# A fused attention and feed-forward kernel: w_out in two tiles, the first relu halved, one sum order exchanged, and fewer score turns in columns 1 and 2

## The chip, the cores and the metric

The kernel runs on one core of a Trainium2 chip. The metric is the device time of one execution in microseconds, the median of several runs. Besides the time there is a hardware profile: one execution with the start and the duration of every instruction on TensorE (PE; its weight loads are PEld), VectorE (DVE), ScalarE (ACT), GpSimd (POOL) and the issuing queues (SP is SyncE), and of every DMA packet.

## The reference

Eight batches of 3008 rows go through a gated attention without softmax, and its result through a feed-forward layer with the activation h cos h:

```python
# u, v: (8, 3008, 256); z: (8, 3008, 64); float32
scores = (1.0 / S) * np.matmul(z, z.transpose(0, 2, 1))
attn = np.maximum(scores, 0.0) ** 2
x = (u * np.matmul(attn, v)).reshape(B * S, D)
# w_in: (256, 2048), w_out: (2048, 256)
h = x @ w_in
out = (h * np.cos(h)) @ w_out
```

The scores are symmetric, because both factors are z.

## The kernel before

Each batch is cut into six columns of 512 rows (J = 0 to 5); the eight batches make 48 slots of one column each. A **score piece** (J, I) holds the 512 x 512 scores of column J against row block I, already through relu and square, as 128 partitions of 2048 fp16 elements. Since the scores are symmetric, piece (I, J) is the transpose of (J, I), and most pieces below the diagonal are not computed but **turned**: a transposing DMA, issued from SyncE, writes the transpose into another buffer. There are 18 such buffers, given out in a fixed order while the program is built.

A score group is two matmul blocks into one of three PSUM banks called E, a relu on ScalarE, and a square on VectorE that writes half a piece:

```python
    def emit_score(later=None):
        b, J, I, h = groups[done_groups[0]]
        ...
            nc.tensor.matmul(
                e[:, t, 0:Wt],
                zT[rows, k * P:(k + 1) * P],
                zT[rows, J * CW:J * CW + Wt],
                start=True,
                stop=True,
            )
        key = (b, J, I)
        a = new_piece(key) if h == 0 else piece(key)
        r = rpool.tile([P, 2, CW], FP16, name="r")
        nc.scalar.activation(r[:, :, 0:W], e[:, :, 0:W], AF.Relu)
        def square():
            ...
                a4 = a.rearrange("p (k w) -> p k w", w=CW)[:, 2 * h:2 * h + 2, 0:W]
                nc.vector.tensor_tensor(a4, r[:, :, 0:W], r[:, :, 0:W], ALU.mult)
        ...
        if cut or (I > J and (b, J, I) not in direct):
            turns.append(((b, I), key))
            turns.sort(key=lambda t: t[0])
            turn_slots[key] = pieces[key]
            pending[pieces[key]] = "held"
```

The list of turns is sorted by the column that will read the result. `emit_turns(due, more)` issues all turns for columns up to `due`, and `more` beyond that. A piece on the diagonal is turned in place by three small DMAs. The buffer of a turned piece is free for a new piece from then on, as soon as its DMA has read it:

```python
    def emit_turns(due, more=0):
        while turns and (turns[0][0] <= due or more > 0):
            if turns[0][0] > due:
                more -= 1
            (b, c), key = turns.pop(0)
            ...
            if I == J:
                ...    # three small transposing DMAs within the piece
            else:
                d = new_piece((b, I, J))
                nc.sync.dma_start_transpose(d.rearrange("p (n j) -> p n j", j=P), a)
            if pending.pop(i) == "dropped":
                free_pieces.append(i)
```

Columns 0, 1 and 2 of the first batch have a phase of their own, which computes all its pieces directly and issues one turn after each row block of columns 1 and 2:

```python
    def phase_a_first(s, n, extra={}):
        ...
            if dh > 0 and (k % 4 == 3):
                drop_piece((b, J, k // 4))
                if s > 0:
                    emit_turns((0, 0), 1)
                    if k < 4:
                        turn_u(s)
                    elif k < 8:
                        for d in range(2):
                            gate_mul(s - 1, d, late_sums.pop(0))
            for _ in range(at.get(i, 0)):
                emit_score(later=squares if s == 0 and i == lo else None)
        if s == 0:
            turn_u(0)
        late_sums.extend(gate_sum(s, *acc[dh]) for dh in range(2))
        hold(late_sums[0][0:1, 0:1])
        load_u(s + 1)
        e_order.append(ea)
```

`gate_sum` adds the two accumulators of one half of the 256 output columns: ScalarE copies one, VectorE adds the other. In column 0 the half dh = 0 is accumulated in the banks M, dh = 1 in a bank E.

From column 3 on, a slot is a `phase_a` (values of one column, with the scores of later columns between them) and a `phase_b` (the feed-forward projections h of the slot before, and the output products of the one before that). `phase_a` calls `emit_turns((b, J))` at its start and `emit_turns(<next column>, 1)` after each score; the `phase_b` after column 2 and all later ones issue one more turn at three places. All stores and all transposing DMAs stand in one queue, SyncE's:

```python
    for s in range(3, NSLOT + 1):
        ...
            phase_a(s)
        ...
            if J == (2 if b > 0 else 3):
                turn_z(b + 1, 1)
        ...
        if s < NSLOT - 2:
            turn_u(s + 2)
        phase_b(s)
```

The head of the kernel casts the first z to fp16, turns it on TensorE, and computes the first scores; filler matmuls keep TensorE going:

```python
    cast_z(nc.vector, 0)
    cast_z(nc.vector, 1)
    cast_z(nc.vector, 2)
    ...
    turn_on_pe(0)
    copy_turned(0)          # on ScalarE; the others on VectorE
    turn_on_pe(1)
    copy_turned(1)
    emit_score(later=squares)
    emit_score(later=squares)
    turn_on_pe(2)
    copy_turned(2)
    squares.pop(0)()
    squares.pop(0)()
    ...
    turn_on_pe(3)
    copy_turned(3)
    filler(2)
    emit_score()
    filler(1)
    emit_score()
    filler(1)
    ...
    phase_a_first(0, 12, {4: lambda: turn_late(4), 8: lambda: turn_late(5)})
    phase_a_first(1, 12)
    nc.gpsimd.dma_start(w_out16, moe_w_out.rearrange("(k p) f -> p k f", p=P))
```

Of the kernel before, what the change touches and what calls it, by code (L numbers as in the profile page):

```python
# [9 lines left out]
FP16 = mybir.dt.float16  # L10
# [4 lines left out]
def kernel(  # L15
# [9 lines left out]
    nc = tc.nc  # L25
    AF = mybir.ActivationFunctionType
# [36 lines left out]
    ppool = pool("ps", 1, space=bass.MemoryType.PSUM)  # L63

    w_in16 = kpool.tile([P, 2, Dff], FP16, name="w_in16")
    w_out16 = kpool.tile([P, NFT, D], FP16, name="w_out16")
    w_mix = kpool.tile([P, 4, NFT // 2, P], FP16, name="w_mix")
    s1, s2, s4 = (kpool.tile([P, NFT // 2, 2 * P], FP16, name=n) for n in ("s1", "s2", "s4"))
    warm = s1[:, 0:2, :].rearrange("p a b -> p (a b)")
# [117 lines left out]
    turn_slots = {}  # L187
    done_groups = [0]

    def emit_score(later=None):  # L190
        b, J, I, h = groups[done_groups[0]]
        done_groups[0] += 1
        cut = I == J and not (b == 0 and J < 3)
        W = 2 * P if cut and h == 0 else width(J)
        zT = zTs[b]
        e = E[take_e()]
        for t in range(2):
            k = 4 * I + 2 * h + t
            half = t if h == 0 else 1 - t
            rows = slice(half * H, (half + 1) * H)  # L200
            Wt = min(W, (2 * h + t + 1) * P) if cut else W
# [7 lines that stand above are left out]
        key = (b, J, I)  # L209
        a = new_piece(key) if h == 0 else piece(key)  # L210
        r = rpool.tile([P, 2, CW], FP16, name="r")
        nc.scalar.activation(r[:, :, 0:W], e[:, :, 0:W], AF.Relu)  # L212
        def square():
            if I > J:
                a4 = a.rearrange("p (k t j) -> p t k j", k=4, j=P)[:, 2 * h:2 * h + 2, :, :]
                r4 = r.rearrange("p t (k j) -> p t k j", j=P)
                nc.vector.tensor_tensor(a4, r4, r4, ALU.mult)  # L217
# [4 lines that stand above are left out]
        if later is None:  # L222
            square()
        else:
            later.append(square)
        if h == 0:
            return
# [11 lines that stand above are left out]
            b, J, I = key  # L239
            i = turn_slots[key]  # L240
            a = piece_bufs[i]
            if I == J:
                a4 = a.rearrange("p (k w) -> p k w", w=CW)
                for rr in range(1, 4):
                    rows = P if J * 4 + rr < NB - 1 else H
                    nc.sync.dma_start_transpose(
                        a4[:, 0:rr, rr * P:rr * P + rows],
                        a[0:rows, rr * CW:rr * CW + rr * P],
# [6 lines that stand above are left out]
# [19 lines left out]
    def gate_sum(s, b0, b1):  # L274
        W = width(s % NC)
        sm = spool.tile([P, CW], FP32, name="sm")
        nc.scalar.copy(sm[:, 0:W], b0[:, 0:W])
        nc.vector.tensor_tensor(sm[:, 0:W], b1[:, 0:W], sm[:, 0:W], ALU.add)  # L278
        return sm
# [75 lines left out]
    def phase_a_first(s, n, extra={}):  # L355
        b, J = s // NC, s % NC
        ea = e_order.pop(0)
        pair = [E[ea][:, 0, :], E[ea][:, 1, :]]
        acc = [pair, M] if s == 1 else [M, pair]
        last = NB - 1  # L360
        run = 1 if s == 0 else 2
        steps = [
            (dh, k)
            for I in range(0, NC, run)
            for dh in range(2)
            for k in range(4 * I, min(4 * (I + run), last))
        ] + [(2, last)]
        lo, hi = 5 if s == 0 else 2, 42
        at = {}
        for i in range(n):  # L370
            p = lo + (hi - lo) * i // (n - 1)
            at[p] = at.get(p, 0) + 1
        for i, (dh, k) in enumerate(steps):
            if i in extra:
                extra[i]()
            if dh == 2:
                emit_value(b, J, last, 0, 0, acc[0][0], False, True)
                emit_value(b, J, last, 1, 1, acc[1][1], False, True)
            else:
                for t in range(2):  # L380
                    emit_value(
                        b, J, k, t, dh, acc[dh][t], k == 0, k == last - 1 and t != dh
                    )
            if dh > 0 and (k % 4 == 3):
                drop_piece((b, J, k // 4))
                if s > 0:
                    emit_turns((0, 0), 1)
                    if k < 4:
                        turn_u(s)
                    elif k < 8:  # L390
# [3 lines that stand above are left out]
                emit_score(later=squares if s == 0 and i == lo else None)  # L394
        if s == 0:
            turn_u(0)
        late_sums.extend(gate_sum(s, *acc[dh]) for dh in range(2))
        hold(late_sums[0][0:1, 0:1])
        load_u(s + 1)
        e_order.append(ea)  # L400
# [51 lines left out]
            )  # L452

    def mix_weights():
        b11, b12 = w_out16[:, 0:F, 0:P], w_out16[:, 0:F, P:D]
        b21, b22 = w_out16[:, F:, 0:P], w_out16[:, F:, P:D]
        t = [w_mix[:, i, :, :] for i in range(4)]
        for dst, p, q in ((t[0], b12, b11), (t[1], b22, t[0]), (t[2], b22, b12), (t[3], b21, t[1])):
            nc.gpsimd.tensor_tensor(dst, p, q, ALU.subtract)
# [5 lines left out]
    def middle(m):  # L465
        acc = M[0][:, 0:D]
        for ft in range(NFT):
            nc.tensor.matmul(  # L468
                acc, gs[m][:, ft, P:T], w_out16[:, ft, :], start=(ft == 0), stop=(ft == NFT - 1)
            )  # L470
        nc.scalar.activation(y_outs[m][0][:, 1, :], acc, AF.Copy, bias=0.0, scale=inv_s2)

    def product(m, n, place):
# [2 lines left out]
        nk = nk // P  # L476
        t = lambda i: w_mix[:, i, :, :]
        left, right = {
            1: (g[:, 0:F, up], w_out16[:, 0:F, 0:P]),
            2: (g[:, F:, up], w_out16[:, F:, 0:P]),  # L480
            3: (s4, w_out16[:, F:, P:D]),
            4: (g[:, F:, low], t(3)),
            5: (s1, t(0)),
            6: (s2, t(1)),
# [46 lines left out]
    def y_block(m, ft, k):  # L531
        final = m == NSLOT - 1
        nc.tensor.matmul(  # L533
            y_bank(m, k),
            gs[m][:, ft, k * P:(k + 1) * P],
            w_out16[:, ft, :],
            start=(ft == 0 and (k % 2 == 0 or (final and k == 3))),
            stop=(ft == NFT - 1 and (k % 2 == 1 or k == mwidth(m) // P - 1 or (final and k == 2))),
        )
# [112 lines left out]
    def cast_z(eng, g):  # L652
        dst = z16s[0][:, 4 * g:4 * g + 4, :].rearrange("p k (t d) -> p k t d", t=2)
        eng.tensor_copy(dst, z32[g].unsqueeze(2).to_broadcast([P, 4, 2, dqk]))
# [7 lines left out]

    def copy_turned(g):
        dst = zTs[0][:, g * CW:(g + 1) * CW]
        if g == 0:
            nc.scalar.copy(dst, turned[g])
        else:
            nc.vector.tensor_copy(dst, turned[g])

    wc = cpool.tile([P, 2, CW], FP16, name="c")  # L670
    nc.scalar.activation(wc[:, 0, 0:P], warm[:, 0:P], AF.Sin)
# [1 line left out]
        nc.tensor.matmul(E[i % 2][:, 0, :], warm[:, 0:P], warm, start=True, stop=True)  # L673
    cast_z(nc.vector, 0)
    cast_z(nc.vector, 1)
    cast_z(nc.vector, 2)
    for g in range(3, NC):
        cast_z(nc.gpsimd, g)
        if g == 3:
# [1 line left out]
    squares = []  # L681
    turn_on_pe(0)
    copy_turned(0)
    turn_on_pe(1)
    copy_turned(1)
    emit_score(later=squares)
    emit_score(later=squares)
    turn_on_pe(2)
    copy_turned(2)
    squares.pop(0)()  # L690
    squares.pop(0)()
    M = [ppool.tile([P, CW], FP32, name=f"M{i}", tag=f"M{i}") for i in range(2)]

    def filler(n):
        for i in range(n):
            nc.tensor.matmul(M[1], warm[:, 0:P], warm, start=True, stop=True)  # L696

    turn_on_pe(3)
    copy_turned(3)
    filler(2)  # L700
    emit_score()
    filler(1)
    emit_score()
# [14 lines left out]

    phase_a_first(0, 12, {4: lambda: turn_late(4), 8: lambda: turn_late(5)})
    phase_a_first(1, 12)  # L720
    nc.gpsimd.dma_start(w_out16, moe_w_out.rearrange("(k p) f -> p k f", p=P))
    for i in range(2):
        emit_h(0, i)()
    phase_a_first(2, 14)
# [65 lines left out]
```

## Time and profile before

| | |
|---|---|
| median of 3 runs | 1193.03 us (1192.85 to 1193.06) |
| span of the profiled execution | 1191.2 us |
| TensorE busy | 1183.7 us, 99% |
| VectorE busy | 1011.5 us, 85% |
| ScalarE, GpSimd busy | 67%, 57% |
| SyncE's queue (turns, stores): time of its packets | 56.6% of 16 DMA engines |
| GpSimd's queue (loads with a cast): time of its packets | 27.7% of 16 DMA engines |

The span runs from the first to the last instruction of the profiled execution. A row of a timeline has the start, the duration, the engine, the line of the kernel, the operation, and the tiles written and read; rows of one group that follow each other are merged (x3). What stands in square brackets is the time that the engine stood idle before it, and what ended it. A row of the waits has the waiting engine and its line, what it waited for, the total, the number and the longest. Two rows of the page carry a digit for each of 40 equal slices of the span, of some 30 us each: the busy share in tenths.

### The profile page before, as it was taken

The page shows a single profiled execution, that of the slowest core. Times are in us where ns is not written, and L with a number is a line of the kernel's source. Part 1 is how long each engine was busy: PE and PEld are TensorE (multiplying, and loading weights), DVE is VectorE, ACT ScalarE, POOL GpSimd, SP SyncE. Part 2 cuts the span into 40 slices and gives each one's busy share as a digit, 9 for nine tenths or more (in the row PEclk, how much of TensorE's full clock was granted, in tenths as well). Part 3 has the DMA queues.
Part 4 walks back from the last instruction along what each step waited for, and adds up shares of the span by engine and source line. Part 5 has one row for each costly group of instructions (what it writes and reads, how often), then busy time and mean ns, then how long its engine had stood idle before and what let it go on. Part 6 is the DMA issues. An engine that isn't in the chain of part 4 may idle for free.

```text
span 1191.2 us, 29044 instructions
## 1 busy us (share of the span) xinstructions
PE 1183.7 (99%) x11887; PEld 726.8 (61%) x11887; DVE 1011.5 (85%) x1302; ACT 794.9 (67%) x927; POOL 679.0 (57%) x717
## 2 busy tenths in 40 slices
PE   9999999999999999999999999999999999999998
PEld 4556665665566656666566665656666566665566
DVE  6888888889988898888988889888888888888776
ACT  7966676667666676667676676666766666666454
POOL 3286745657466573755647556476555655545452
PEclk9999999999999999999999999999999999999999
DMA  9999999569995799955999469984798837974301
GB/s 160 175 172 158 115 171 130 102 122 104 173 127 101 123 137 166 126 89 103 155 152 130 86 106 158 168 123 70 120 162 152 122 72 120 173 122 84 65 20 54
DMA packets 449142, 148.00 MB, mean 124 GB/s; under 512 B 401264, under 2 KB 432496, under 8 KB 449008
## 3 DMA queue, kind: packets, MB, share of 16 engines
q1 hardware_dynamic: 368464, 112.93, 56.6%
q0 software_dynamic: 80032, 32.78, 27.7%
q8 instruction: 93, 1.52, 0.5%
q10 hardware_dynamic: 512, 0.43, 0.1%
q14 instruction: 41, 0.34, 0.1%
HBM read 66.32 MB, written 24.64 MB: 76 GB/s over the span
## 4 chain that ended last, share of the span: by engine, by line
PE 98%; ACT 1%; DVE 1%; issue 0%; POOL 0%; DVEq 0%; ACTq 0%
PE E L412 27%; PE M L490 23%; PE M L266 20%; PE E L266 19%; PE E L202 6%; PE M L533 1%; ACT r L212 1%; PE M L468 1%; DVE g L423 0%; PE E L673 0%; DVE sm L278 0%; PE E L533 0%; POOL s L441 0%; PE M L696 0%; ACT c L420 0%
## 5 line engine op out<-in xcount | busy, mean ns | idle before, releaser
L420 ACT ACTIVATE c<-E 128x1024 f16<-128x1024 f32 (+1 forms) x384 | 385.7, 1007 | 216.4 <-PE E L412 214.1
L423 DVE SCALAR_TENSOR_TENSOR g<-E,c 128x1024 f16<-128x1024 f32 (+1 forms) x384 | 458.9, 1197 | 62.0 <-ACT c L420 60.9
L212 ACT ACTIVATE r<-E 128x512 f16<-128x512 f32 (+1 forms) x342 | 328.0, 967 | 112.3 <-PE E L202 106.6
L266 PEld LDWEIGHTS <-v 64*128 64x128 f16 x4512 | 245.7, 94 | 229.6 <-issue 18.8
L412 PE MATMUL E<-x,w_in 128*128 128x512 f16 (+1 forms) x1408 | 354.0, 375 | 0.0
L441 POOL TENSOR_TENSOR s<-g 128x512 f16<-128x512 f16 (+1 forms) x184 | 207.8, 1130 | 189.3 <-DVE g L423 139.4
L266 PE MATMUL M<-A,v 64*128 64x512 f16 (+1 forms) x2256 | 283.0, 372 | 0.0
L266 PE MATMUL E<-A,v 64*128 64x512 f16 (+1 forms) x2256 | 278.0, 371 | 0.0
L442 POOL TENSOR_TENSOR g<-g 128x512 f16<-128x512 f16 (+1 forms) x184 | 219.0, 1190 | 14.4
L412 PEld LDWEIGHTS <-w_in 128*128 128x128 f16 x1536 | 133.1, 98 | 108.9 <-issue 19.5
L490 PEld LDWEIGHTS <-g 128*128 128x128 f16 x2816 | 172.5, 98 | 40.8
L217 DVE TENSOR_TENSOR A<-r 128x1024 f16<-128x1024 f16 x240 | 173.2, 734 | 15.1 <-ACT r L212 14.3
L294 POOL TENSOR_TENSOR x<-sm,uT 128x512 f16<-128x512 f32 (+1 forms) x43 | 48.6, 1131 | 223.5 <-DVE sm L278 223.5
L490 PEld LDWEIGHTS <-s 128*128 128x128 f16 x2112 | 129.4, 98 | 32.1 <-DVE s L448 0.5
L202 PE MATMUL E<-zT 64*128 64x512 f16 (+4 forms) x684 | 128.0, 356 | 1.6 <-DVE sm L278 0.7
L448 DVE TENSOR_TENSOR s<-s,g 128x1024 f16<-128x1024 f16 (+1 forms) x92 | 99.7, 1085 | 2.1 <-POOL s L441 2.1
L490 PE MATMUL M<-w_mix,s 128*128 128x128 f16 x1408 | 94.0, 219 | 0.3 <-POOL s L441 0.3
L490 PE MATMUL M<-w_mix,g 128*128 128x128 f16 x1408 | 93.6, 219 | 0.0
L490 PE MATMUL M<-w_out,g 128*128 128x128 f16 x1408 | 93.6, 219 | 0.0
L220 DVE TENSOR_TENSOR A<-r 128x512 f16<-128x512 f16 (+1 forms) x102 | 80.1, 785 | 8.6 <-ACT r L212 7.6
L202 PEld LDWEIGHTS <-zT 64*128 64x128 f16 x684 | 38.7, 94 | 38.4 <-issue 3.8
L450 DVE TENSOR_TENSOR s<-g,s 128x1024 f16<-128x1024 f16 (+1 forms) x92 | 60.6, 661 | 0.0
(58 smaller groups left out, 636.3 us busy)
## 6 DMA issues: line engine op xcount, KB each, us to landing
out_dram<-o SPq DMA_DIRECT2D x87, 256.0 KB, 2.1
v<-in_v_dram POOLq DMA_DIRECT2D x40, 256.0 KB, 11.5
u<-in_u_dram POOLq DMA_DIRECT2D x40, 256.0 KB, 4.5
A<-A SPq DMA_TRANSPOSE x252, 5.3
z<-in_z_dram POOLq DMA_DIRECT2D x14, 192.0 KB, 10.9
z<-in_z_dram POOLq DMA_DIRECT2D x14, 176.0 KB, 6.8
v<-in_v_dram POOLq DMA_DIRECT2D x8, 192.0 KB, 16.1
u<-in_u_dram POOLq DMA_DIRECT2D x8, 192.0 KB, 3.7
```

The costliest lines, as they stand in the source:

```text
L202: nc.tensor.matmul(e[:, t, 0:Wt], zT[rows, k * P:(k + 1) * P], zT[rows, J * CW:J * CW + Wt], start=True, stop=True,)
L212: nc.scalar.activation(r[:, :, 0:W], e[:, :, 0:W], AF.Relu)
L217: nc.vector.tensor_tensor(a4, r4, r4, ALU.mult)
L220: nc.vector.tensor_tensor(a4, r[:, :, 0:W], r[:, :, 0:W], ALU.mult)
L266: nc.tensor.matmul(bank[:, 0:width(J)], vs[b, k // 4][t * H:(t + 1) * H, k % 4, dh * P:(dh + 1) * P], value_rhs(b, J, k, t), start=start, ...
L412: nc.tensor.matmul(e[:, f, 0:W], w_in16[:, k, ft * P:(ft + 1) * P], x[:, k, 0:W], start=(k == 0), stop=(k == 1),)
L420: nc.scalar.activation(c[:, :, 0:W], e[:, :, 0:W], AF.Sin, bias=half_pi, scale=inv_s2)
L423: return lambda: nc.vector.scalar_tensor_tensor(gs[m][:, 2 * i:2 * i + 2, 0:W], e[:, :, 0:W], 1.0, c[:, :, 0:W], ALU.mult, ALU.mult)
L441: nc.gpsimd.tensor_tensor(s1[:, f, 0:n], g[:, f, low], g[:, lower, low], ALU.add)
L442: nc.gpsimd.tensor_tensor(g[:, f, low], g[:, f, up], g[:, f, low], ALU.subtract)
L448: nc.vector.tensor_tensor(s2[:, f, 0:n], s1[:, f, 0:n], g[:, f, up], ALU.subtract)
L490: nc.tensor.matmul(acc[:, k * P:(k + 1) * P], left[:, ft, k * P:(k + 1) * P], right[:, ft, :], start=(ft == 0 and k == 0), stop=(ft == F - ...
```

## The change

It has four parts. **w_out** is loaded into two tiles of eight row blocks each, by two DMAs, so that the first products need only the first. **The head**: the first turned z is copied by VectorE, the third cast moves behind that copy, the relu of the first score group is halved between ScalarE and VectorE and its square follows in two halves, and one filler matmul is left out. **The sum order of column 0**: the sum that frees the E bank is made first. **The turns**: in columns 1 and 2 only those pieces are turned that column 3 needs; the others follow where the later phases call for them. The purpose is an earlier start of the first column, a shorter turnover to the second one, and DMA queues left to the loads of the first phases.

```diff
-    w_out16 = kpool.tile([P, NFT, D], FP16, name="w_out16")
+    w_out16 = [kpool.tile([P, NFT // 2, D], FP16, name=f"w_out{i}") for i in range(2)]
 ...
-    def emit_score(later=None):
+    def emit_score(later=None, shared=False):
 ...
-        nc.scalar.activation(r[:, :, 0:W], e[:, :, 0:W], AF.Relu)
+        if shared:
+            r2 = rpool.tile([P, 2, CW], FP16, name="r")
+            nc.scalar.activation(r[:, 0, :], e[:, 0, :], AF.Relu)
+            nc.vector.tensor_scalar_max(r2[:, 0, :], e[:, 1, :], 0.0)
+        else:
+            nc.scalar.activation(r[:, :, 0:W], e[:, :, 0:W], AF.Relu)
+
         def square():
-            if I > J:
+            if shared:
+                for t, rt in enumerate((r, r2)):
+                    dst = a[:, (2 * h + t) * CW:(2 * h + t + 1) * CW]
+                    nc.vector.tensor_tensor(dst, rt[:, 0, :], rt[:, 0, :], ALU.mult)
+            elif I > J:
 ...
                 if s > 0:
-                    emit_turns((0, 0), 1)
+                    emit_turns((0, 3))
 ...
-        late_sums.extend(gate_sum(s, *acc[dh]) for dh in range(2))
+        sums = {dh: gate_sum(s, *acc[dh]) for dh in ((1, 0) if s == 0 else (0, 1))}
+        late_sums.extend(sums[dh] for dh in range(2))
 ...  (every use of w_out16 takes the half that it needs)
     def copy_turned(g):
         dst = zTs[0][:, g * CW:(g + 1) * CW]
-        if g == 0:
-            nc.scalar.copy(dst, turned[g])
-        else:
-            nc.vector.tensor_copy(dst, turned[g])
+        nc.vector.tensor_copy(dst, turned[g])
 ...
-    cast_z(nc.vector, 2)
 ...
     copy_turned(0)
+    cast_z(nc.vector, 2)
     turn_on_pe(1)
     copy_turned(1)
+    emit_score(later=squares, shared=True)
     emit_score(later=squares)
-    emit_score(later=squares)
+    squares.pop(0)()
     turn_on_pe(2)
     copy_turned(2)
     squares.pop(0)()
-    squares.pop(0)()
 ...
-    filler(2)
+    filler(1)
 ...
-    nc.gpsimd.dma_start(w_out16, moe_w_out.rearrange("(k p) f -> p k f", p=P))
+    w_rows = moe_w_out.rearrange("(i k p) f -> i p k f", p=P, k=F)
+    for i in range(2):
+        nc.gpsimd.dma_start(w_out16[i], w_rows[i])
```

## The prediction, made before the run

> **What bounds the kernel now.** I first read the busy table and the slices of the page, then TensorE's waits, then the timeline of the stretches that the change touches.
>
> ```profile
> PE 1183.7 (99%) x11887; PEld 726.8 (61%) x11887; DVE 1011.5 (85%) x1302; ACT 794.9 (67%) x927; POOL 679.0 (57%) x717
> ...
> DMA  9999999569995799955999469984798837974301
> ```
>
> TensorE is busy for 1183.7 of 1191.2 us, so 7.5 us in all are open. The DMA row holds a 9 in its first seven slices (about 30 us each): moving a transfer there pushes another. TensorE's waits, all of them:
>
> ```profile
> PE E L673 <- DVE s L636: 1.2, 1, 1.2
> PE E L202 <- DVE sm L278: 0.7, 1, 0.7
> PE E L202 <- DVE g L423: 0.4, 1, 0.4
> PE M L490 <- POOL s L441: 0.3, 1, 0.3
> PE E L202 <- ACT zT L666: 0.3, 1, 0.3
> PE E L202 <- DVE zT L668: 0.2, 1, 0.2
> ```
>
> The reader sees that no wait on a DMA is among them, although the queues are full: every transfer that TensorE needs has landed before it asks. All that can be won is here too: 0.7 at the end of column 0 (line 278), 0.3 at the first copy (line 666). What can be lost is read from the queue that issues the turns (SyncE) and from VectorE, at columns 3 and 4:
>
> ```profile
> 74.21 1.86 SPq L252 DMA_TRANSPOSE A<-A  x1
> 76.16 1.58 SPq L559 DMA_DIRECT2D out_dram<-o  x2
> 77.85 2.43 SPq L141 DMA_TRANSPOSE zT<-z  x1
> 80.38 1.42 SPq L168 DMA_TRANSPOSE uT<-u  x1
> 81.90 3.77 SPq L246 DMA_TRANSPOSE A<-A  x3
> 85.77 3.58 SPq L252 DMA_TRANSPOSE A<-A  x1
> ...
> 98.16 1.00 SPq L559 DMA_DIRECT2D out_dram<-o  x2
> ```
>
> ```profile
> 83.18 0.42 DVE L220 TENSOR_TENSOR A<-r 128x512 f16<-128x512 f16 x1
> 83.51 0.69 DVE L450 TENSOR_TENSOR s<-g,s 128x1024 f16<-128x1024 f16 x1
> 84.12 0.62 DVE L220 TENSOR_TENSOR A<-r 128x896 f16<-128x896 f16 x1
> 84.65 0.68 DVE L278 TENSOR_TENSOR sm<-E,sm 128x512 f32<-128x512 f32 x1
> ```
>
> Columns are start, duration, engine, line, operation. The queue issues nearly without a pause, one behind the other. The first VectorE row writes the first half of score piece (column 5, row block 5); the sum in the last row frees the third E bank.
>
> **What the Trainium skill says.** "TensorE: Matmul & The Clock Gate", section "Wait — 56ns, not 53.3ns?": matmuls of 512 columns start every 426.7 ns on a cold array, every 215.7 ns on a warm one. The trace agrees: 427 ns between the warming matmuls up to 4.15 us, 216 ns from 6.9 us on. So the very first scores run cold, and starting them earlier gains less than it seems. "DMA: Bandwidth & Descriptors", section "Queues, rings and completion order": a DMA engine serves its queues in turn, packet by packet. The trace agrees: a whole-piece turn issued at 74.21 landed after 4.3 us with the load queue empty, the one at 85.77 after 8.3 us beside the z loads. "SBUF — State Buffer", section "SBUF: two separate sides": VectorE and GpSimd share a port pair under a lock. The squares at 76.93 and 78.49 took 1.64 us beside GpSimd's sums against 0.68 at 81.97; the change leaves this as it is.
>
> **The change part by part.**
>
> *Head.* The copy of the first turned z goes from ScalarE (0.59 us, 4.82 to 5.41) to VectorE (0.42, as its other copies). VectorE has its first two casts done by 4.24, and the third moves behind the copy. First score at 5.30 instead of 5.46: 0.16 gained. The first relu, 1.02 us on ScalarE, becomes two halves of 512 columns: ScalarE about 0.6 (as the 512-wide copy of line 277), VectorE about 0.65 (as the sum of line 278, 0.68). One of four filler matmuls goes (0.22), so the first value matmul may start near 8.4 instead of 8.75. But VectorE now holds a chain from 4.82: five copies and one cast at 0.42, the half relu at 0.65, four squares at 0.7 to 0.8, about 6.1 us to the copy that ends near 10.95 and that in turn releases the last turn on TensorE. Before, that copy (10.53) ended at 10.95 as well. Of the 0.35 I keep 0.3.
>
> *End of column 0.* TensorE's score at 25.07 waited for the second of two sums (23.74 and 24.34, 0.68 each), because that one frees its E bank. With the order exchanged it is released after the first, at 24.42: 0.6 gained. Bank M, then freed second at 25.0, is needed at about 25.1. Sum so far: 0.9 us.
>
> *w_out in two tiles.* The load was issued at 39.09 and landed after 14.4 us at 53.5; the first use is at 54.6. It hides before; with halves and fewer turns beside it, it lands earlier. Worth 0, but it keeps the 0.9 us from running into it.
>
> *The turns.* Before, columns 1 and 2 issue ten whole-piece turns; after, three: (0,3), (1,3), (2,3). Of the other seven, all for columns 4 and 5, three go to the phase after column 2, before the two stores of the first result, and four fall behind them. (3,5) joins those four; (4,5) was there already. In the order of instructions after the change, SyncE's queue from the first store on is: two stores, first half of zT, uT of slot 4, turn (3,4), turn (0,5), three small turns of the diagonal piece (4,4), turn (1,5), and so on. The column 5 pieces are needed only at about 121 us, so as data they are early enough. As **buffers** they are not: with 18 buffers, the scores (5,5) are now given the buffer of piece (1,5), and VectorE's square of them waits for the semaphore of that very turn. Before, the buffer of (2,5) was used, whose turn was issued at 70.31 and landed 4.4 us later, at 74.7, far ahead of 83.18.
>
> When does turn (1,5) land? The first store needs ScalarE's copy of line 565 (70.48, the first of two, 0.59): 71.1, less the 0.9 gained, 70.2. From there, by the rows shown: stores 1.00, zT 2.43, uT 1.42, two whole turns 2 x 1.86, diagonal 3.77, sum 12.3, and about 0.1 between each, together 13.1. So it is issued at 83.3 at the earliest. Landing takes 4.3 us in a quiet queue (87.6), 8.3 us beside the z loads of the second half (91.6), which run at the same time. I take T = 90.5.
>
> VectorE would have come to that square at 83.18 - 0.9 = 82.3, so it stands for about 8 us. From the square to the end of the sum that frees the third E bank are 2.15 us (83.18 to 85.33). TensorE takes that bank with the third projection group of the phase, at 86.81, or 85.9 after the gain. So it resumes at T + 2.15 = 92.65 and loses 92.65 - 85.9 = **6.7 us**. Nothing gives it back, since TensorE is the bound afterwards. Sum: -0.9 + 6.7 = +5.8, 1193.0 + 5.8 = 1198.8 us.
>
> **The rivals.** (a) *Only the gain*: the turns run faster than I add up, or the queue gets ahead, and VectorE doesn't stand. For it: the queues have less to do up to 55 us. Against: the store that heads the queue can't start before 71.1 - 0.9 whatever stands before it, and the issue durations are measured. This gives 1192.1. (b) *Quiet landing*: the z loads start earlier, because the first half of zT lands earlier, and are done before: T = 87.6, loss 3.9, 1196.0. (c) *The backlog goes on*: behind (1,5) stand three more whole turns, the diagonal (5,5), and the second half of zT, which the score at 105.03 reads, and the stores of the next result. I count its issue near 101 to 103 and landing near 107; with TensorE already 5.8 us late the score comes at 110.8, so it is hidden. If loads slow the queue by 4 us more, it costs as much again: up to 1203. (d) *VectorE as the bound of the head*: its added half relu and cast eat the 0.3; this costs no more than that.
>
> **Range and chances.** The size hangs on T, between 87.6 and about 94: 1195.7 to 1202.3; widened by 0.5 at each side for the gain and for (c). I give (a) one chance in ten. Two per cent are 24 us; neither the gain nor a stall in one place reaches that, unless (c) repeats in each batch, which the order of instructions speaks against: from the fourth column on, both kernels turn the same pieces at the same places.
>
> **What would show it.** In the profile after: among VectorE's waits a new one of 5 to 10 us on the DMA A, at a square of 512 columns near 82 us; TensorE's third projection group after column 3 coming late by 4 to 8 us, with its wait put down to the sum of line 288; SyncE issuing turn (1,5) at 83 or later and landing in 4 to 9 us. Steps of the head: first score near 5.3, and the wait of 0.7 at the end of column 0 down to 0.1. From column 5 on, every phase should have its old length and a constant shift. I am wrong if VectorE doesn't wait there, if the turn lands before 84, or if TensorE loses time in other places, such as on pieces of columns 4 and 5 that come late as data.

## The result, and the profile after

The changed kernel takes 1203.26 us (median; 1202.01 to 1203.72), the kernel before 1192.94 in the same runs: ratio 1.0082, 95% interval 1.0069 to 1.0095. By the ratio that is 9.8 us slower, by the medians 10.3. The predicted direction and cause were right; the predicted loss of 5.8 us was too small.

TensorE's waits, all of them (waiting engine and line, what for, total, number, longest):

```profile
PE E L423 <- DVE sm L288: 7.8, 1, 7.8
PE E L681 <- DVE s L647: 1.2, 1, 1.2
PE E L202 <- DVE g L434: 0.4, 1, 0.4
PE M L501 <- POOL s L452: 0.3, 1, 0.3
PE E L202 <- DVE zT L676: 0.2, 1, 0.2
```

The 0.7 us at the end of column 0 is no longer there, and one new wait of 7.8 us is. VectorE's timeline shows where it comes from:

```profile
81.90 0.68 DVE L461 TENSOR_TENSOR s<-g,s 128x1024 f16<-128x1024 f16 x1
92.07 0.42 DVE L230 TENSOR_TENSOR A<-r 128x512 f16<-128x512 f16 x1 [9.49 <-DMA A<-A]
92.41 0.68 DVE L461 TENSOR_TENSOR s<-g,s 128x1024 f16<-128x1024 f16 x1
93.02 0.62 DVE L230 TENSOR_TENSOR A<-r 128x896 f16<-128x896 f16 x1
93.55 0.68 DVE L288 TENSOR_TENSOR sm<-E,sm 128x512 f32<-128x512 f32 x1
```

The square of 512 columns is the first half of the scores (5,5). It stood for 9.49 us for a transposing DMA, and the three operations behind it stood with it, down to the sum that frees the third E bank. SyncE's queue, first the two stores, then what stood between them and turn (1,5), the first of the four at 87.50:

```profile
70.87 1.57 SPq L570 DMA_DIRECT2D out_dram<-o  x2
72.55 1.72 SPq L141 DMA_TRANSPOSE zT<-z  x1
74.37 1.91 SPq L168 DMA_TRANSPOSE uT<-u  x1
76.39 7.20 SPq L262 DMA_TRANSPOSE A<-A  x2
83.68 3.78 SPq L256 DMA_TRANSPOSE A<-A  x3
87.50 9.92 SPq L262 DMA_TRANSPOSE A<-A  x4
```

Turn (1,5) was issued at 87.50 and landed 4.5 us later, at 92.0: the moment at which VectorE goes on. Last, TensorE's timeline at that place, and its granted clock by stretches (the stretch; its length; busy time of each engine; then clock, DMA share, GB/s):

```profile
84.62 1.03 PE L423 MATMUL E<-x,w_in 128*128 128x512 f16 x4
85.48 1.06 PE L501 MATMUL M<-w_out,g 128*128 128x128 f16 x16
94.29 1.86 PE L423 MATMUL E<-x,w_in 128*128 128x512 f16 x4 [7.75 <-DVE sm L288]
```

```profile
86.50:94.20 7.70, 0.04 (x1) 0.00 (x0) 2.13 (x5) 0.48 (x2) 0.00 (x0) 0.64 1.16 196
94.20:98.00 3.80, 3.71 (x21) 2.40 (x21) 2.33 (x4) 1.02 (x1) 2.49 (x3) 0.50 1.16 215
98.00:102.00 4.00, 4.00 (x41) 2.67 (x40) 3.08 (x4) 1.91 (x2) 2.41 (x4) 0.88 0.49 96
```

Four matmuls of 512 columns take 1.86 us after the wait and 1.03 before it: TensorE comes back at half clock, and is at full clock again only near 99. Each matmul can be matched with the same one of the kernel before; the difference of their starts is the lag. The changed kernel is 0.44 us ahead until 85.5. The third projection group starts 7.48 us behind, at 94.29; in the kernel before it is this row:

```profile
86.81 1.03 PE L412 MATMUL E<-x,w_in 128*128 128x512 f16 x4
```

So the wait cost 7.9. By the time the clock is back the lag is 9.73, so the half clock cost 2.25 more. From there to the last slot the lag stays between 9.72 and 9.74 us. One place holds the whole loss.

### The profile page after: what moved, and what is told of

Its sections match the earlier page's. It is cut to its first block, busy times and chain, and to the rows that moved or that the text cites. A ratio compares the mean times of both kernels' runs of the same rounds, so it can differ in the third digit from the quotient of the medians.

```text
span 1201.2 us, 29042 instructions
## 1 busy us (share of the span) xinstructions
PE 1186.4 (99%) x11886; PEld 728.5 (61%) x11886; DVE 1012.0 (84%) x1305; ACT 793.3 (66%) x926; POOL 679.4 (57%) x718
## 5 line engine op out<-in xcount | busy, mean ns | idle before, releaser
L217 ACT ACTIVATE r<-E 128x1024 f16<-128x1024 f32 x341 | 326.9, 966 | 111.9 <-PE E L202 106.0
L453 POOL TENSOR_TENSOR g<-g 128x512 f16<-128x512 f16 (+1 forms) x184 | 219.0, 1190 | 14.4
L227 DVE TENSOR_TENSOR A<-r 128x1024 f16<-128x1024 f16 x240 | 173.0, 733 | 14.4 <-ACT r L217 13.7
L230 DVE TENSOR_TENSOR A<-r 128x1024 f16<-128x1024 f16 (+1 forms) x101 | 78.8, 781 | 18.0 <-DMA A<-A 9.5
## 6 DMA issues: line engine op xcount, KB each, us to landing
z<-in_z_dram POOLq DMA_DIRECT2D x14, 192.0 KB, 10.3
```

Source lines behind the costliest of these rows:

```text
L453: nc.gpsimd.tensor_tensor(g[:, f, low], g[:, f, up], g[:, f, low], ALU.subtract)
```

## Experiments

The theory: the loss is the reuse of one buffer. The scores (5,5) may not be written before turn (1,5) has read that buffer, and the deferral put this turn far back in SyncE's queue. Its rival: the deferred traffic itself is too much for the queues of columns 3 and 4, whichever buffer is used. A second rival: w_out in two tiles, or the head, has a part in it.

**1 and 2: the deferral undone, and the deferral alone.**

```diff
 # 1: in the changed kernel        # 2: in the kernel before
-  emit_turns((0, 3))              -  emit_turns((0, 0), 1)
+  emit_turns((0, 0), 1)           +  emit_turns((0, 3))
```

> The whole change, but columns 1 and 2 turn one piece after each row block as the kernel before does. If the deferred turns make the whole loss (buffer theory and traffic theory alike), VectorE no longer waits for a turn near 82 us and the time is the kernel before less the 0.44 us that the changed kernel was ahead when column 3 began: 1192.5. If w_out in two tiles or the head had a part in it, more than 1193.5.

> The kernel before with only the deferred turns. If they alone make the loss: TensorE waits 7 to 8 us at the third projection group after column 3 and runs at half clock for some 4.6 us afterwards, 10.2 us in all: 1203.2. If the loss needs the earlier start of the other parts too, less than 1200.

Measured: 1 takes 1.0007 of the time before (0.9998 to 1.0015), 2 takes 1.0078 (1.0062 to 1.0095). So the deferral alone makes nearly the whole loss, and without it the loss is gone. The stop in 2 is the same one, shorter than the 7 to 8 us expected:

```profile
PE E L412 <- DVE sm L278: 5.9, 1, 5.9
```

But 1 is no faster than before, though 0.44 us were expected; its median, 1194.33, lies past the 1193.5 that was to tell of a part of the second rival. TensorE's waits in 1 have two rows that neither parent has:

```profile
PE M L544 <- DVE sm L288: 1.1, 1, 1.1
PE M L276 <- DVE o L514: 0.5, 1, 0.5
```

The first ends at 55.6, in the phase after column 2, and costs 1.2 us; the next experiments show what that is. The second ends at 97.9 and costs 0.6. Experiment 5 has it too, so here the second rival has a small part: it comes with the head or the two tiles of w_out when the turns are as before. Its cause is followed no further than to GpSimd, for which VectorE stood 1.35 us in 1 and 1.50 in 5.

**3: another buffer.** The deferral stays, the order of the turns stays; only the buffer of (5,5) changes. The second index leaves the piece (5,4) in the buffer that it had; from the next batch on, buffers 10 and 13 have changed places.

```diff
-        pieces[key] = free_pieces.pop(0)
+        pieces[key] = free_pieces.pop(free_pieces.index(10) if key == (0, 5, 5) else 1 if key == (0, 5, 4) else 0)
```

> The whole change with the deferred turns, issued in the same order; only the scores (5,5) get buffer 10, whose last readers are TensorE's values of column 3, instead of buffer 13 of the turned piece (1,5). Buffer theory: VectorE's wait of 9.5 us is gone and with it the half clock. What may stay: the second half of zT lands near 106, and the score that reads it comes at 104.6, so up to 1.6 us; 1192.5 to 1194.5. Traffic theory (the later turns clog the queue and TensorE lacks their data): the loss stays, over 1199.

Measured: 1.0061 of before (1.0046 to 1.0076). The buffer theory as I had put it falls: VectorE's wait is gone, and most of the loss is not. TensorE's one new wait of over 0.4 us, SyncE's queue, and TensorE at that place:

```profile
PE E L202 <- DMA zT<-z: 4.3, 1, 4.3
```

```profile
85.35 11.80 SPq L262 DMA_TRANSPOSE A<-A  x4
97.20 4.32 SPq L256 DMA_TRANSPOSE A<-A  x3
101.74 1.48 SPq L141 DMA_TRANSPOSE zT<-z  x1
```

```profile
103.99 1.03 PE L276 MATMUL E<-A,v 64*128 64x512 f16 x8
109.34 0.61 PE L202 MATMUL E<-zT 64*128 64x512 f16 x2 [4.33 <-DMA zT<-z]
109.75 1.49 PE L276 MATMUL E<-A,v 64*128 64x512 f16 x6
```

The second half of zT stands behind four whole and three small turns; it is issued at 101.74, lands 7.6 us later, and the score that reads it stands for 4.33. The half clock follows here too: the lag grows from 4.3 to 5.9 us after the wait ends. In the changed kernel this wait was hidden: the second half of zT landed at 106.2 there (issued at 102.54, 3.7 us), and TensorE, 9.7 us late, came to that score only near 114.8. So both the buffer and the backlog are real, the first hides the second, and removing the first alone brings out the second. (The backlog removed and the buffer kept was not run.) The profiled run is the fastest of the four, 1198.89 us; the others, 1199.73 to 1201.43, have no profile, so up to 2.5 us of their loss are not located.

**4: the wait filled.** To separate the half clock from the wait, TensorE gets work for its idle time:

```diff
+            if s == 3 and i == 2:
+                for _ in range(35):
+                    nc.tensor.matmul(M[0], w_in16[:, 0, 0:P], w_in16[:, 0, 0:CW], start=True, stop=True)
             times_c = emit_h(m, unit)
```

> The whole change, with 35 matmuls of 512 columns on unused data put ahead of the third projection group after column 3, where TensorE stands for 7.75 us; their result is overwritten.[...] If the half clock after the wait costs 2.4 us of the 10.2 (idle theory), TensorE keeps its clock, and the time falls by 2.4 against the changed kernel, to 1200.6. If the half clock were not from the idle stretch, or cost nothing, the time stays at 1203 or rises.

Measured: 1200.1 us, 1.0059 of before (1.0044 to 1.0074). The 35 matmuls, 216 ns apart, kept TensorE busy for 7.45 of the 7.70 us before 94.20. The stretch after the wait, which had clock 0.50 and 21 matmuls in the changed kernel:

```profile
94.20:98.00 3.80, 3.80 (x43) 2.67 (x41) 3.76 (x6) 2.05 (x2) 2.61 (x3) 1.00 1.35 163
```

Clock 1.00 and 43 matmuls. In the lag this kernel loses 7.96 us at the wait and nothing after it, against 7.9 and 2.25: the half clock comes from the idle time.

**5, 6 and 7: head and sum order apart.** 5 is the changed kernel with sum order and turns as before. 6 is the kernel before with

```diff
-        late_sums.extend(gate_sum(s, *acc[dh]) for dh in range(2))
+        sums = {dh: gate_sum(s, *acc[dh]) for dh in ((1, 0) if s == 0 else (0, 1))}
+        late_sums.extend(sums[dh] for dh in range(2))
```

and 7 is 6 with the head's copy on VectorE, the cast behind it and one filler less, but with a whole first relu.

> The kernel before with the changed head and w_out in two tiles; sum order and turns as before. In the changed kernel the first value matmul came at 8.739 (8.749 before) and the end of column 0 was 0.16 us later, because VectorE's half relu stands 0.64 us for ScalarE's half and its chain runs late. If so: 0.16 us slower, 1193.1. If the prediction's 0.3 gain was there and lost elsewhere: 1192.6.

> The kernel before with only the order of the two sums of column 0 exchanged. The score that waits at 25.07 is released by the first sum: 0.6 us faster, 1192.3, and the whole rest of the trace shifted by 0.6. If something behind it (bank M, ScalarE) takes the wait over, less than 0.2.

> The kernel before with the sum order exchanged and of the changed head only the copy on VectorE, the third cast behind it and one filler less; the first relu stays whole on ScalarE and the squares in their old order. If the halved relu is what lost the head's gain: first score at 5.30, first value matmul near 8.6, and 0.15 us more than the sum order alone: 1192.2. If VectorE's cast behind the copy is what delays the head, no gain over the sum order alone.

Measured: 5 takes 0.9996 of before (0.9988 to 1.0004), which decides nothing; in its profile it is 0.3 us ahead until 96 and 0.4 behind after the second stop of experiment 1. 6 takes 1.0021 (1.0013 to 1.0029) and 7 takes 1.0025 (1.0012 to 1.0038): against the expectation both are *slower* by 2.5 to 3 us. The matched matmuls show the sum order's gain of 0.6 us at 25.07 in 6, in 7, and in every other profile that has it. Both kernels are ahead until 54 us, 6 by 0.8 and 7 by 0.6. Then, at the first products with w_out, these waits of 6:

```profile
DVE A L217 <- DMA A<-A: 3.3, 1, 3.3
```

```profile
PE M L534 <- DVE sm L278: 1.7, 1, 1.7
...
PE M L534 <- DMA w_out<-in_moe_w_out_dram: 0.4, 1, 0.4
```

and of 7:

```profile
PE M L534 <- DMA w_out<-in_moe_w_out_dram: 2.5, 1, 2.5
```

w_out landed 16.0 us after its issue in 6, 18.3 in 7, and 14.4 in the kernel before, where it was 1.2 us ahead of its use. And VectorE's square of (3,5) waits for a turn, again one that reads the buffer it is to fill; with the turns issued one by one this is turn (0,5). It landed at 54.4 in 6 and 52.7 in 7, and at 48.2 in the kernel before, some 4 us ahead of the square. The 1.1 us of experiment 1 have the same cause: there the same square stood for 2.08 us and began at 53.69, and turn (0,5) had landed at 53.60. Half clock follows in 6 and 7 as well (0.50 to 0.60 from 56.5 to 60). So the sum order wins its 0.6 us and loses some 4 to transfers that were on time by 1 and 4 us. Why a start that is less than 1 us earlier delays them so much stays open.

This is what the deferral and the two tiles of w_out are for, and it takes both: w_out's halves landed after 6.5 and 9.0 us in the changed kernel, after 10.0 and 15.2 in 1, which has the two tiles without the deferral, and the whole w_out after 14.5 in 2, which has the deferral without the two tiles.

**8: w_out early instead.** If that reading holds, an earlier load does the same without the deferral. 8 is 7 with the load of w_out moved:

```diff
+    nc.gpsimd.dma_start(w_out16, moe_w_out.rearrange("(k p) f -> p k f", p=P))
     phase_a_first(1, 12)
-    nc.gpsimd.dma_start(w_out16, moe_w_out.rearrange("(k p) f -> p k f", p=P))
```

> Sum order exchanged and unhalved head as in the run before, turns as in the kernel before, w_out in one tile; its load is issued after column 0 (near 25 us) instead of after column 1 (38.3). If that run lost its 0.6 to 1.0 us of gain, and 3 to 4 more, only because w_out (landing after 18.3 us) and the turn (0,5), whose buffer the scores (3,5) reuse, share the DMA engines at 38 to 57 us: both waits gone, w_out down before 40, and 1192.2 to 1192.6. If the gain is lost to the earlier start itself, 1195 or more again.

Measured: 1192.6 us, 0.9993 of before (0.9985 to 1.0001), and no wait for w_out or a turn on TensorE or VectorE. One moved line takes some 4 us off experiment 7.

**9 and 10: both stops removed.** 9 is experiment 3 with the turn of the second half of zT moved ahead of the turns (2,5), (3,5), (4,5) and (5,5); 10 is 9 with a whole first relu.

```diff
                 emit_turns(divmod(s + 1, NC), 1)
+                if s == 3 and done_groups[0] == 44:
+                    turn_z(1, 1)
 ...
-            if J == (2 if b > 0 else 3):
+            if b > 0 and J == 2:
                 turn_z(b + 1, 1)
```

> The whole change with the other buffer for the scores (5,5), and the turn of the second half of zT moved in SyncE's queue ahead of the turns (2,5), (3,5), (4,5) and (5,5), which are needed only at 121 us. If the backlog of that queue is all that was left of the loss: TensorE's wait of 4.3 us for zT and the half clock after it are gone, and with buffer and queue order mended the deferral costs nothing: 1192.4 to 1193.2. If the deferred turns cost in themselves, something else waits and it stays over 1196.

> The same, with the first relu whole on ScalarE and the squares in their old order. If the halved relu costs the head 0.2 to 0.3 us: 0.2 to 0.3 faster than the run before this. If the head's differences of 0.2 to 0.4 between profiles come from when TensorE's clock rises, no difference that can be told.

Measured: 9 takes 1192.61 us, 0.9991 of before (0.9985 to 0.9997); 10 takes 1192.72, 0.9991 (0.9983 to 0.9999). SyncE's queue in 9, with the turn of zT second:

```profile
84.73 3.26 SPq L262 DMA_TRANSPOSE A<-A  x1
88.23 2.38 SPq L141 DMA_TRANSPOSE zT<-z  x1
90.70 7.66 SPq L262 DMA_TRANSPOSE A<-A  x3
98.45 4.09 SPq L256 DMA_TRANSPOSE A<-A  x3
```

It lands 5.6 us after 88.23, at 93.8, ten microseconds before its use, and no wait of TensorE's is over 0.4 us but the one at its start. The same bytes are turned, through the same queue; one buffer number and one place in the order make the difference between 10 us lost and 0.5 to 1 us won. These two are the versions whose intervals lie below the kernel before as well.

## Why the prediction was right, and where it was off

*The cause* held by name: one new wait of VectorE's at a square of 512 columns for turn (1,5), the stop of the third projection group put down to line 288, a constant lag after it. The time lies past the point predicted, and the median 0.5 us past the upper end of the range (1202.3 and the 0.5 of widening), because the sum had one term too few and one of the wrong size. In the lag: 5.8 us by the prediction's sum, 1.6 more because the bank came free later, 2.25 for the missing term, together 9.7. The gain before the wait is no part of it: what TensorE is ahead, it only waits longer. (The range's lower end, 1195.7, should be 1196.0 by the same sum.)

*The term that was missing* is the half clock: 2.25 us. The prediction had TensorE go on at full speed after the wait. It had cited the Trainium skill's page "TensorE: Matmul & The Clock Gate" for the cold rate, but not drawn the conclusion; the page's section "What's actually happening" gives about 3.4 us of idle time after which the clock falls to half, and about as much busy time until it rises. The traces agree for the long waits (7.75 and 4.33 us idle, then 0.50), but here less was enough. In the changed kernel the clock fell at 88.7, some 2.2 us into the wait: this is the 0.64 of the stretch from 86.50 to 94.20. The 2.54 us idle in 7 were followed by 0.50, and so were 0.38 and 1.70 us in 6, with two matmuls between them. The wait of 1.06 us in 1 was not. In these traces the time between two changes of the clock is always a multiple of 3.41 us: 81.92 at full and 10.24 at half clock in the changed kernel, 102.4 and 3.41 in 3, 51.2 and 3.41 in 6 and 7. So where a wait falls in these steps probably matters beside its length; no run tests that.

*The landing of turn (1,5)*: 90.5 predicted, 92.0 measured, 1.5 us more lost. That it is no more is partly luck, for two larger errors stand against each other. The turn was issued at 87.50 and not at 83.3. The queue started at 70.87 rather than 70.2, and the two whole turns (3,4) and (0,5) took 7.20 us, not 2 x 1.86: 1.79 for the first and 5.32 for the second, which was issued at 78.27, just ahead of the z loads (from 78.85 on). The landing itself was then quiet, 4.5 us, where I had set 7.2: the z loads had landed by 87.3. I put the slowness at the wrong member of the queue.

*The gain before it*: 0.9 predicted, 0.44 in the profile. The sum order's term was right, 0.6 against 0.59. The head's 0.3 came out as -0.15. Part of it is the halved relu. VectorE's half did not run beside ScalarE's; it waited for it:

```profile
6.58 0.69 DVE L215 TENSOR_SCALAR r<-E 128x512 f16<-128x512 f32 x1 [0.64 <-ACT r L214]
```

The instruction waits for ScalarE's semaphore, though the two halves are different matmul blocks of the E buffer and are only read. But the head can't be judged by one profile: the matmuls after the first two score groups start anywhere from 5.60 to 6.43 us, depending on when TensorE's clock rises (at 4.15 us in 4, at 6.78 in the changed kernel). The first value matmul comes at 8.54 to 8.75 in three profiles with the old head, 8.28 to 8.75 in six with the changed one, 8.37 to 8.59 in three with the unhalved one. 9 and 10 took the same time. What the head is worth stays open within 0.3 us.

*w_out in two tiles* was given 0, as a guard. That was right for this kernel, and too little was made of it: 6 and 7 show that without it and the deferral the 0.6 us turn into a loss of 2.5 to 3.

*Rival (c)*, the backlog, was listed as hidden up to 4 us: it was hidden, and 3 laid it bare. *Rival (a)* is out: the turn did not land by 84. *Rival (b)* was half right: the z loads were done before the turn and its landing was quiet, as it says, but the turn ahead of it had run beside the loads and taken 5.32 us, so it landed at 92.0 and not at 87.6. No stall repeated in later batches.

## What to carry to other kernels

A deferred transfer moves two dates: when its result is there, and when the buffer it reads is free; look up who is next to get that buffer. In an in-order queue, what is deferred stands in front of everything issued later, so sort the queue by the time of use and not by what is easy to emit. Where every transfer lands just in time, a small gain upstream must be bought together with an earlier load, and a long wait on TensorE (here, from some 2 us on) is to be counted with the half clock that follows it.

## What the runs showed that I had not expected

After idle stretches of 7.75, 4.33 and 2.54 us TensorE's granted clock was 0.50 for another 3.2 to 4.7 us; after 1.06 us it stayed at 1.00. A wait of 7.9 us therefore cost 10.2, and filling it with 35 idle matmuls won 2.2 of them back in the lag. And the same load, the whole of w_out, landed after 14.4, 16.0 and 18.3 us in kernels that differ by less than 1 us at its issue; turn (0,5), beside it, after 9.2, 15.8 and 13.9.
